# Start of a fused pooled attention and two MLPs: attention of nine subtiles in fp32, value sums on GpSimd, one table of preparation

## The chip, the cores and the metric

The kernel runs on one core of one Trainium2 chip. The metric is the device time of one execution in microseconds; a program's time is the median of its runs.

## The reference

Attention with pooled keys and values over 8 batches of 8 heads, then two MLPs over all 4608 tokens:

```
k_p = k.reshape(B, H, S // 8, 8, D).mean(axis=3)          # B 8, H 8, S 576, D 64
v_p = v.reshape(B, H, S // 8, 8, D).mean(axis=3)
attn = softmax(q @ k_p.T / sqrt(D));  x = attn @ v_p       # x: 4608 x 512
h = x @ w_in                                               # w_in 512 x 2048
g = where(h >= 1, h, where(h <= -1, 0, (h + 1) ** 2 / 4))
y = g @ w_out                                              # w_out 2048 x 512
h2 = y @ w_in2;  out = (h2 * sigmoid(h2)) @ w_out2
```

q, k and v are fp32, the four weights are 64-bit and are converted on the chip.

## The kernel before, in words

Products of the MLPs are made of three f16 products each (`three`, L121: high by high, high by low, low by high), so every weight and every activation is held as a high and a low f16 part. A *split* (L348) makes the two: ScalarE writes the high part (L349), VectorE the low part (L350).

The 4608 tokens are worked on in nine tiles of 512, and a tile's attention in four *subtiles* of 128 tokens. A batch has 576 tokens, so subtiles 0 to 8 (1152 tokens) are those of batches 0 and 1, and subtile 4 has tokens of both. A subtile passes five stages: `att_qT` (queries transposed, L523), `att_scores` (L546), `att_norm` (softmax, L585), `att_T` (transposed weights, L601) and `att_pv` (output, split into x of its tile, L632).

Before the change the first four subtiles (i < NI = 4) go in fp32: TensorE transposes queries and weights by the identity (L529, L607), multiplies with fp32 keys (L559) and fp32 sums of values (L647), and ScalarE copies the results from PSUM. All other subtiles go in f16: queries, keys, values and weights are split, and the queries, keys and weights are transposed by DMAs that SP issues (L544, L490, L612). For that the key sums and value sums of a batch need a mean (ScalarE, L448), a maximum over the partitions (`all_max`, L106: a product with the identity and a VectorE reduction), and a split (`batch_keys` L483, `batch_values` L499).

Sums over eight rows: keys of batch 0 by a VectorE reduction per head (L425), values of batch 0 by 64 products with the identity (L434) and one ScalarE copy (L439), the other batches by a DMA that accumulates, issued by GpSimd (`kv_more`, L412), and two VectorE additions (L442, L445).

A weight piece is read as raw 64-bit words. `look` takes its maximum (VectorE, L113), `scales` or `search` works out powers of two by a run of VectorE operations on a few columns (`w_scale` L167, `bits` L99), and the conversion is ScalarE L183, VectorE L95 and L191, ScalarE L261 (w_in) or L215 (w_out), a ScalarE cast to the high part (L263, L220) and a GpSimd subtraction for the low part (L264, L221). w_in has nine pieces, w_out four column blocks of two.

Tile 0 runs: attention of subtiles 0 to 3; 16 chunks of `emit_h` (L799, products `hps`) with their evacuation (ScalarE L817, VectorE L95, ScalarE L824, VectorE L828, then the split L856 and L857), whose results are all kept; then 4 x 16 steps of `yA` (L859, products `y`) that need the converted w_out blocks; then `evac_yA` (L876). Conversions, sums of batches 0, 1 and 2 and the attention of subtiles 4 to 7 are put between (L1108 to L1193). PSUM for attention is a ring of six buffers in the first part and of two (`ps_a`) after it (`att_ps`, L381).

The other tiles (L1214) do both MLP steps in one loop, with one or two steps of attention each turn and the second MLP's weights prepared beside. From L1270 the second MLP runs over tiles of 256 tokens.

The order on each engine: the code is traced in program order, and a planner that models the engines then lays out each engine's queue from it; each engine takes its queue in order. `behind(...)` (L128) keeps the instructions of a block from being laid out ahead of the latest *anchor* on the named engines. SP and GpSimd issue the DMAs.

Of the kernel before, what the change touches and what calls it, by code (L numbers as in the profile page):

```python
# [34 lines left out]
def tile_pooled_attention_two_mlps(  # L35
# [22 lines left out]
    POOL = 8  # L58
    SP = S // POOL
# [42 lines left out]

    ident = const.tile([128, 128], F32, name="ident")
# [57 lines left out]
    def all_of(m):  # L161

        g = sm.tile([128, 1], F32, tag="wg", name="wg", bufs=3)
        all_max(g, m)
        return g

    def w_scale(e, d, s, g, up=14):  # L167


        t = sm.tile([128, 8], F32, tag="wt", name="wt", bufs=2)  # L170
# [24 lines left out]
    def steps(piece, dst, scale, loaded, fill=None):  # L195
# [17 lines left out]
        def s3():  # L213
# [5 lines left out]
            hi, lo, *end = dst()  # L219
            nc.scalar.copy(out=hi, in_=x)  # L220
            nc.gpsimd.tensor_tensor(out=lo, in0=x, in1=hi, op=ALU.subtract)  # L221
            for f in end:
                f()
# [3 lines left out]
    def new_scale(e, g):  # L227
        ds = sm.tile([128, 2], F32, tag="ws", name="ws", bufs=3)
        w_scale(e, ds[:, 0:1], ds[:, 1:2], g)
        return ds[:, 0:1], ds[:, 1:2]  # L230

    def weight_in(w, e, tiles, cuts, rooms):
# [4 lines left out]
        mx, s, g, down = col(n), col(n), col(n), col(n)  # L237
# [16 lines left out]
        def work(p):  # L254
# [9 lines left out]
            nc.gpsimd.tensor_tensor(out=lo, in0=x, in1=hi, op=ALU.subtract)  # L264
# [39 lines left out]
    def weight_whole(w, e, fill, pieces):  # L304
# [16 lines left out]
        def scale():  # L321
            m = sm.tile([128, 1], F32, tag="wm1", name="wm1", bufs=3)
            nc.vector.tensor_reduce(out=m, in_=mx, axis=AX.X, op=ALU.max)
            w_scale(e, down, s, all_of(m), 12)
# [40 lines left out]
    SPT = (SP + 15) // 16 * 16  # L365
    v16 = [bp.tile([SP, 2, H, D], F16, name=f"v16{j}") for j in range(2)]
    e16 = [bp.tile([128, 2, 4, 128], F16, name=f"e16{j}") for j in range(2)]
# [6 lines left out]
    k32 = bp.tile([128, NP, 2, SP], F32, tag="kT", name="k32", bufs=2)  # L374
    nc.vector.memset(k32, 0.0)
    for x in e16:
        nc.gpsimd.memset(x, 0.0)
# [39 lines left out]

    def kv_pool(b, which, j):
        if j == 0:
# [3 lines left out]
        if (b, which) == (0, "k"):  # L423
            for h in (2 * j, 2 * j + 1):
                nc.vector.tensor_reduce(  # L425
                    out=sums[b, which][0:SP, h], in_=kv_raw.pop((b, which, h)).rearrange("p r d -> p d r"),
                    axis=AX.X, op=ALU.add,
                )
        elif b == 0:
            if j == 0:  # L430
                kv_raw["ps"] = att_ps([SP, H, D])
# [697 lines left out]
    r = XT[0]  # L1129
# [184 lines left out]
```

## Time and profile before

| | |
|---|---|
| median of 3 runs | 1617.79 us (1617.38 to 1619.02) |
| profiled execution | 1619.99 us, its span 1618.2 us |
| TensorE busy | 1535.0 us (95%) |
| VectorE busy | 1170.4 us (72%) |
| ScalarE busy | 898.9 us (56%) |
| GpSimd busy | 563.2 us (35%) |
| DMA | 166.35 MB, mean 103 GB/s |

PE is TensorE (PEld its weight load), DVE VectorE, ACT ScalarE, POOL GpSimd, SP the queue that issues most DMAs. A row's L number is a line of the kernel; a helper has one line for all that call it, so rows are told apart by their tiles as well. TensorE is busy nearly all the time from about 280 us on; the part before that is where the share is lower.

### The profile page before, as it was taken

To read this page: it belongs to the slowest core of one execution; us is meant where nothing else is said; L and a number is where in the kernel's file an instruction comes from. 1 tells how busy PE (TensorE), PEld (TensorE's weight loads), DVE (VectorE), ACT (ScalarE), POOL (GpSimd) and SP (SyncE) were. 2 spreads that over 40 slices of the span, in tenths; PEclk is the share of its full clock that TensorE was granted. 3 is DMA by queue.
4 is the path that set the end of the run, shared out by engine and by line. 5 is a ranking of instruction groups with operands and counts; after the bars stand their busy time and mean duration, and the time that the engine had idled before them with its cause. 6 is when DMAs were issued, how large, how long until landed. Compare 5 with 4: busy or idle time off the path is not lost.

```text
span 1618.2 us, 34378 instructions
## 1 busy us (share of the span) xinstructions
PE 1535.0 (95%) x14278; PEld 1060.2 (66%) x14278; DVE 1170.4 (72%) x2154; ACT 898.9 (56%) x1418; POOL 563.2 (35%) x508
## 2 busy tenths in 40 slices
PE   6846789999999999999999999999999999999998
PEld 6522344444444444444444489999999999999998
DVE  5798668676767677766757667777777777777765
ACT  2686565556666675664666555444455444555543
POOL 2314431214324333221555333343443333443322
PEclk9887799999999999999999999999999999999999
DMA  9635989957759576447583330100000100000000
GB/s 294 129 84 127 169 161 191 175 123 137 143 105 172 108 144 116 108 100 193 165 317 134 127 131 28 35 33 28 28 28 28 36 33 28 28 28 29 28 15 28
DMA packets 226157, 166.35 MB, mean 103 GB/s; under 512 B 154960, under 2 KB 193616, under 8 KB 226000
## 3 DMA queue, kind: packets, MB, share of 16 engines
q1 hardware_dynamic: 216592, 155.88, 37.8%
q0 software_dynamic: 9408, 8.27, 4.1%
q8 instruction: 112, 1.84, 0.5%
q14 instruction: 45, 0.37, 0.1%
HBM read 102.76 MB, written 33.55 MB: 84 GB/s over the span
## 4 chain that ended last, share of the span: by engine, by line
PE 56%; DVE 12%; issue 9%; ACT 8%; DMA 7%; POOL 7%; SPq 1%; DVEq 0%; POOLq 0%; ACTq 0%
PE y L122 6%; PE y L124 6%; PE y L123 6%; PE hps L123 5%; PE hps L124 5%; PE hps L122 5%; POOL c L714 4%; PE y L1018 3%; PE y L1020 3%; PE y L1019 3%; PE hb L123 3%; PE hb L122 3%; PE hb L124 3%; DMA yin<-y 3%; DVE g L350 2%
## 5 line engine op out<-in xcount | busy, mean ns | idle before, releaser
L124 PE MATMUL hb<-xh,wc 128*128 128x128 f16 x2016 | 347.7, 219 | 0.0
L122 PE MATMUL hb<-xh,wc 128*128 128x128 f16 x2016 | 347.7, 219 | 0.0
L123 PE MATMUL hb<-xl,wc 128*128 128x128 f16 x2016 | 347.7, 219 | 0.0
L350 DVE SCALAR_TENSOR_TENSOR g<-c,small,g 128x512 f16<-128x512 f32 x252 | 228.6, 910 | 94.4 <-ACT g L349 94.4
L1018 PE MATMUL y<-wd,g 128*128 128x256 f16 x1008 | 274.9, 273 | 1.7 <-DVE ob L1031 1.6
L1020 PE MATMUL y<-wd,g 128*128 128x256 f16 x1008 | 274.9, 273 | 0.0
L1019 PE MATMUL y<-wd,g 128*128 128x256 f16 x1008 | 274.9, 273 | 0.0
L958 ACT ACTIVATE c<-c,small 128x512 f32<-128x512 f32 x144 | 103.2, 717 | 230.4 <-DVE c L955 230.4
L122 PE MATMUL y<-g,wb 128*128 128x512 f16 x544 | 210.2, 387 | 19.9 <-ACT wb L220 19.9
L349 ACT ACTIVATE g<-c,small 128x512 f16<-128x512 f32 x252 | 177.6, 718 | 85.7 <-POOL c L717 48.2
L122 PE MATMUL hps<-xh,wa 128*128 128x512 f16 x576 | 219.9, 382 | 4.3 <-ACT wa L263 1.8
L123 PE MATMUL hps<-xl,wa 128*128 128x512 f16 x576 | 220.1, 382 | 1.4 <-DVE xl L350 1.4
L124 PE MATMUL hps<-xh,wa 128*128 128x512 f16 x576 | 219.6, 382 | 1.2 <-POOL wa L264 1.2
L124 PE MATMUL y<-g,wb 128*128 128x512 f16 x544 | 209.8, 386 | 3.6 <-POOL wb L221 3.6
L123 PE MATMUL y<-g,wb 128*128 128x512 f16 x544 | 210.3, 387 | 1.0 <-DVE g L857 1.0
L123 PEld LDWEIGHTS <-wc 128*128 128x128 f16 x2016 | 197.1, 98 | 2.4
L122 PEld LDWEIGHTS <-wc 128*128 128x128 f16 x2016 | 197.1, 98 | 2.2
L955 DVE TENSOR_TENSOR c<-c,hb 128x512 f32<-128x512 f32 x252 | 168.2, 682 | 41.5 <-PE hb L124 39.3
L124 PEld LDWEIGHTS <-wc 128*128 128x128 f16 x2016 | 197.1, 98 | 0.0
L828 DVE SCALAR_TENSOR_TENSOR g<-g,small,u 128x512 f32<-128x512 f32 x144 | 126.4, 878 | 61.8 <-ACT u L824 59.9
L593 POOL TENSOR_TENSOR e<-e,den 128x576 f32<-128x576 f32 x36 | 53.1, 1475 | 324.6 <-DVE den L592 234.5
L714 POOL TENSOR_TENSOR c<-c 128x512 f32<-128x512 f32 x108 | 163.9, 1532 | 2.8
(171 smaller groups left out, 2683.1 us busy)
## 6 DMA issues: line engine op xcount, KB each, us to landing
raw<-in_moe_w_out_dram SPq DMA_DIRECT2D x21, 1024.0 KB
raw<-in_moe_w_in_dram SPq DMA_DIRECT2D x18, 1024.0 KB
y<-y SPq DMA_DIRECT2D x36, 256.0 KB
yin<-y SPq DMA_DIRECT2D x18, 512.0 KB
out_dram<-ob SPq DMA_DIRECT2D x36, 256.0 KB
d<-hl SPq DMA_DIRECT2D x32, 256.0 KB
qt<-in_q_dram SPq DMA_DIRECT2D x31, 256.0 KB
wc<-d SPq DMA_DIRECT2D x8, 896.0 KB
```

What stands on the lines that cost most here:

```text
L122: nc.tensor.matmul(out=acc, lhsT=wh, rhs=xh, start=start, stop=False)
L123: nc.tensor.matmul(out=acc, lhsT=wh, rhs=xl, start=False, stop=False)
L124: anchor["pe"] = nc.tensor.matmul(out=acc, lhsT=wl, rhs=xh, start=False, stop=stop)
L349: a = nc.scalar.activation(out=hi, in_=x, func=AF.Copy, scale=s)
L350: return a, nc.vector.scalar_tensor_tensor(out=lo, in0=x, scalar=s, in1=hi, op0=ALU.mult, op1=ALU.subtract)
L714: nc.gpsimd.tensor_tensor(out=out, in0=a, in1=b, op=ALU.subtract)
L828: anchor["dve"] = nc.vector.scalar_tensor_tensor(out=g32_t[s], in0=g32_t[s], scalar=r["br"], in1=u_t.pop(s), op0=ALU.subtract, op1=ALU.max)
L955: nc.vector.tensor_tensor(out=out, in0=x, in1=y, op=ALU.add)
L958: nc.scalar.activation(out=x, in_=x, func=AF.Silu, scale=r["c1"])
L1018: nc.tensor.matmul(out=acc, lhsT=xh, rhs=wh, start=start, stop=False)
L1019: nc.tensor.matmul(out=acc, lhsT=xh, rhs=wl, start=False, stop=False)
L1020: nc.tensor.matmul(out=acc, lhsT=xl, rhs=wh, start=False, stop=stop)
```

## The change

- Subtiles 0 to 8 (`NE = 2 * S // 128 = 9`) go in fp32, not 0 to 3. Batch 1 gets fp32 keys (`keys32(1)`, a second `k32`), and the sums of values of batches 0 and 1 stay fp32, in the room of `v16`. `batch_keys` and `batch_values` of batches 0 and 1 fall away. The room of `e16` serves as a third buffer of `e` for subtiles 2 and 5.
- Batch 0's values are summed by GpSimd in three halvings for each half of the heads, traced at the first step; key heads 3 and 6 likewise.
- 16 products of the identity with itself are traced ahead of everything else on TensorE.
- Small columns (scales and maxima of w_in's pieces, `e1`, `wt`, `den`, `ch`) lie two columns apart.
- The preparation of tile 0 (looks, scales, conversions, sums of batch 1, w_out steps, attention slots) is put by tables of steps, `tick`. Three low halves (w_in pieces 3 and 7, w_out piece 0) are subtracted by VectorE. The first 40 attention slots of the later loop get `behind`.
- `cyb` shares the room of `m1`; `wm1` too.

```diff
+    WARM = 16
+    V0_AT = 0
+    VM_AT = 3
+    K_POOL = (3, 6)
+    LOOK_AT = [-6, -5, -4, -4, -3, -3, -2, -2, -1]
+    SCALE_AT = [-6, -3, -2, -1]
+    C1_AT = [-6, -3, -2, 2, 2, 3, 4, 10, 12]
+    B1_AT = [3, 4, 5, 6, 11]
+    MORE2_AT = 13
+    W2_AT = [[7, 10, 12, 13, 17, 18], [19, 19, 19, 19, 19, 19], [21, 21, 21, 21, 23, 23], [27, 27, 27, 27, 27, 27]]
+    SLOTS_AT = [9, 10, 12, 13, 14, 17, 18, 19, 20, 20, 23, 24, 28, 29, 30, 31, 31, 31, 31, 32]
+    HELD = 40
+    LO1 = (3, 7)
+    LO2 = (0,)
...
-    cols, free = const.tile([128, 96], F32, name="cols"), iter(range(96))
+    cols, free, free2 = const.tile([128, 136], F32, name="cols"), iter(range(46)), iter(range(45))
+    spread = cols[:, 46:136].rearrange("p (n u) -> p n u", u=2)
...
+    def apart(n):
+        i = [next(free2) for _ in range(n)][0]
+        return spread[:, i:i + n, 0]
...
+    def halving(to, r):
+
+        plus(r[:, 0:4], r[:, 0:4], r[:, 4:8])
+        plus(r[:, 0:2], r[:, 0:2], r[:, 2:4])
+        plus(to, r[:, 0], r[:, 1])
...
-            for n in range(POOL):
-                nc.tensor.matmul(
-                    out=ps[:, 2 * j:2 * j + 2], lhsT=ident[0:SP, 0:SP], rhs=r[:, :, n], start=n == 0,
-                    stop=n == POOL - 1,
-                )
-            if j == 3:
-                nc.scalar.copy(out=sums[b, which][0:SP], in_=kv_raw.pop("ps"))
+            if j < 2:
+                r = kv_raw.pop((b, which, j)).rearrange("p h r d -> p r h d")
+                halving(sums[b, which][0:SP, 4 * j:4 * j + 4], r)
...
-            for p in range(2 * hf, 2 * hf + 2) if i < NI else ():
-                nc.tensor.matmul(
-                    out=ps[:, p % 2 * 2:p % 2 * 2 + 2], lhsT=qT[:, p], rhs=k32[:, p], start=True, stop=True
-                )
+            for p in range(2 * hf, 2 * hf + 2) if i < NE else ():
+                for o, n, b, _ in segs(i):
+                    nc.tensor.matmul(
+                        out=ps[o:o + n, p % 2 * 2:p % 2 * 2 + 2], lhsT=qT[:, p, o:o + n], rhs=k32[b][:, p],
+                        start=True, stop=True,
+                    )
...
+    def warm(n):
+        ps = att_ps([128, 128])
+        for _ in range(n):
+            nc.tensor.matmul(out=ps, lhsT=ident, rhs=ident, start=True, stop=True)
...
     kv_load(0, "k")
+    warm(WARM)
...
+    def tick(n):
+        for f in steps_at.get(n, ()):
+            with behind("pe", "act", "dve"):
+                f()
+        if n >= 0:
+            slots_to(sum(a <= n for a in SLOTS_AT))
...
+        tick(n - 8)
...
-        2: lambda: keys_mean(0), 3: lambda: batch_keys(0), 4: lambda: batch_values(0), 5: lambda: sums_of(1, "k"),
-        6: lambda: keys_mean(1), 7: lambda: batch_keys(1), 8: lambda: sums_of(1, "v"),
-        9: lambda: values_mean(1), 10: lambda: batch_values(1),
...
+        tick(s + 1)
     new_acc(0)
     for d in range(KD):
-        if d + 1 < KD:
-            for n in range(6):
-                w2step(d + 1, n)
         for m in range(KF):
-            if m % 4 == 3:
-                slots_to(4 + 4 * d + m // 4 + 1)
+            if m % 4 == 0:
+                tick(KF + 3 + 4 * d + m // 4)
             yA(m, d, m == 0, m == KF - 1)
```

## Rows read from the trace of the kernel before

**Rows 1.** Windows: stretch, length, busy us (x instructions) by engine, granted clock, DMA share, GB/s.

```profile
0.00:60.00 60.00, 42.90 (x233) 36.97 (x234) 37.75 (x82) 21.77 (x33) 12.02 (x19) 0.96 0.98 256
60.00:127.00 67.00, 41.90 (x178) 18.25 (x176) 59.84 (x105) 56.18 (x80) 17.77 (x11) 0.81 0.42 107
127.00:215.00 88.00, 65.80 (x431) 30.01 (x432) 62.02 (x145) 48.76 (x77) 37.47 (x26) 0.79 0.73 137
215.00:300.00 85.00, 78.14 (x527) 37.90 (x524) 67.88 (x160) 49.77 (x88) 19.96 (x20) 0.96 0.91 183
300.00:950.00 650.00, 645.14 (x4012) 311.11 (x4011) 451.84 (x854) 398.09 (x652) 226.68 (x230) 1.00 0.62 148
950.00:1618.00 668.00, 661.11 (x8910) 625.94 (x8907) 491.05 (x812) 324.34 (x492) 249.26 (x204) 1.00 0.09 30
```

**Rows 2.** Timeline, 0 to 60 us: start, us, engine, line, operation, idle before.

```profile
5.85 0.35 PE L469 MATMUL att<-ident,sum 72*128 72x72 f32 x1 [5.85 <-DVE sum L425]
...
19.64 1.11 PE L529 MATMUL early<-ident,q 128*128 128x128 f32 x4 [0.76 <-DMA q<-in_q_dram]
...
28.06 13.88 PE L434 MATMUL att<-v,ident 72*72 72x128 f32 x64
...
42.93 0.46 DVE L568 TENSOR_REDUCE mx<-early 128x4 f32<-128x288 f32 x1 [6.94 <-PE early L559]
...
47.33 0.69 ACT L349 ACTIVATE xh<-att,small 128x512 f16<-128x512 f32 x1 [0.53 <-DVE den L589]
...
59.85 1.01 PE L122 MATMUL hps<-xh,wa 128*128 128x512 f16 x2 [1.25 <-ACT xh L349]
```

**Rows 3.** Waits of PE, 60 to 215 us: total us, times, longest.

```profile
PE y L122 <- ACT wb L220: 19.9, 2, 14.9
```

**Rows 4.** The chain that ended last, 60 to 215 us: start, us, what.

```profile
155.76 9.27 DMA aT<-e
...
165.94 2.32 SPq L544
...
169.00 11.93 DMA qT<-rows
```

**Rows 5.** Groups by line on POOL, 0 to 215 us: busy us, mean ns, idle before.

```profile
L264 POOL TENSOR_TENSOR wa<-xf,wa 128x1024 f16<-128x1024 f32 x7 | 16.1, 2296 | 16.5 <-ACT wa L263 16.4
L593 POOL TENSOR_TENSOR e<-e,den 128x576 f32<-128x576 f32 x8 | 10.0, 1251 | 60.4 <-DVE den L592 43.3 <-DVE eq L95 16.7 <-DVE wt L97 0.4
```

**Rows 6.** Groups by line on DVE, 60 to 215 us.

```profile
L350 DVE SCALAR_TENSOR_TENSOR krows<-sum,skv,krows 80x512 f16<-80x512 f32 x3 | 2.5, 838 | 0.9 <-ACT krows L349 0.9
```

**Rows 7.** Timeline: attention products in fp32 and f16, and f16 products of the MLP.

```profile
21.48 1.33 PE L559 MATMUL early<-k,qT 128*128 128x144 f32 x4
...
47.56 0.66 PE L647 MATMUL early<-aT,sum 72*64 72x128 f32 x8
...
49.08 1.04 PE L607 MATMUL early<-ident,e 128*72 128x128 f32 x8
...
147.48 0.69 PE L554 MATMUL att<-kT,qT 128*128 128x72 f16 x16 [0.28 <-DMA qT<-rows]
...
203.73 0.86 PE L647 MATMUL att<-aT,v 72*64 72x128 f16 x24
...
700.85 0.38 PE L124 MATMUL y<-g,wb 128*128 128x512 f16 x1
...
702.57 0.38 PE L123 MATMUL y<-g,wb 128*128 128x512 f16 x1
```

**Rows 8.** Timeline: small VectorE operations that start while GpSimd runs.

```profile
61.99 2.43 POOL L264 TENSOR_TENSOR wa<-xf,wa 128x1024 f16<-128x1024 f32 x1 [4.88 <-ACT wa L263]
62.35 2.10 DVE L97 TENSOR_SCALAR wt<-cols 128x3 f32<-128x3 f32 x1
...
130.23 2.57 POOL L264 TENSOR_TENSOR wa<-xf,wa 128x1024 f16<-128x1024 f32 x1
130.74 0.20 DVE L95 TENSOR_SCALAR wm<-wm 128x1 f32<-128x1 f32 x1
```

More of the change, by code (lines that the diff above doesn't have):

```diff
@@ L236, in weight_in @@
         held, n = {}, len(cuts)
-        mx, s, g, down = col(n), col(n), col(n), col(n)
+        mx, s, g, down = (apart(n) for _ in range(4))
         def load(p):
@@ L373, in tile_pooled_attention_two_mlps @@
     nc.gpsimd.memset(vm, FLOOR * POOL / (H * D))
[L374 to L377, printed above, removed]
+    k32 = [bp.tile([128, NP, 2, SP], F32, tag="kT", name="k32", bufs=2) for _ in range(2)]
+    nc.vector.memset(k32[0], 0.0)
+    nc.gpsimd.memset(k32[1], 0.0)
     early = {"n": 0, "on": True}
@@ L492, in values_mean @@
     def values_mean(b):
-        sums_mean(sums[b, "v"][0:SP], vm, v16[b % 2])
+        junk = v16[b % 2] if b > 1 else ap.tile([SPT, H, 2, D], F16, tag="krows", name="by", bufs=2)[0:SP]
+        sums_mean(sums[b, "v"][0:SP], vm, junk)
     def values_scale(b):
@@ L534, in att_qT @@
             return
-        e, s = (sm.tile([128, 1], F32, tag=n, name=n) for n in ("eq", "sq"))
-        c = cq_t[i] = sm.tile([128, 1], F32, tag="cq", name="cq", bufs=3)
+        c = sm.tile([128, 3], F32, tag="cq", name="cq", bufs=3)
+        e, s, c = (c[:, j:j + 1] for j in range(3))
+        cq_t[i] = c
         x = rows(128)
@@ L552, in att_scores @@
                 for o, n, b, _ in segs(i):
-                    for j in range(2) if i >= NI else ():
+                    for j in range(2) if i >= NE else ():
                         nc.tensor.matmul(
@@ L595, in att_norm @@
         )
-        for hf, x in enumerate(e16 if i >= NI else ()):
+        for hf, x in enumerate(e16 if i >= NE else ()):
             x, y = x[:, :, :, 0:SP], e[:, 4 * hf:4 * hf + 4]
@@ L776, in small @@
     def small(**names):
-        x = sm.tile([128, sum(names.values())], F32, tag="t" + "".join(names), name="small", bufs=3)
-        r, a = {}, 0
+        wide = names.pop("ch", 0)
+        x = sm.tile([128, sum(names.values()) + 2 * wide], F32, tag="t" + "".join(names), name="small", bufs=3)
+        r, a = {"ch": x[:, 0:2 * wide].rearrange("p (n u) -> p n u", u=2)[:, :, 0]}, 2 * wide
         for n, w in names.items():
@@ L1201, in next_slot @@
     def next_slot():
-        slots_left.pop(0)()
+        if len(slots_left) > NTOKS - HELD:
+            with behind("pe", "act", "dve"):
+                slots_left.pop(0)()
+        else:
+            slots_left.pop(0)()
         q_to(2 * NI + (NTOKS - len(slots_left)) // 4 + 3)
```

139 lines of the change are left out of this document (66 added, 73 removed).

## Prediction

> **What bounds the kernel now.** I read the windows view first, cut at the points where the work changes: the attention of the first token tile (0 to 60 us), the first half of tile 0's network (60 to 127), its second half (127 to 215), tile 1 (215 to 300), the other tiles (300 to 950), the second network (950 to 1618) [rows 1]. From 300 us on TensorE is busy for 645.14 of 650 and 661.11 of 668 us at a granted clock of 1.00. The diff touches that part only in small columns, so what is won or lost before 300 us should reach the end one for one. Before 300 us TensorE is idle for 17.1, 25.1, 22.2 and 6.9 us of the four stretches, and its granted clock is 0.81 and 0.79 in the two that hold tile 0. That is the room: some 71 us idle, and products that run at half speed for part of the time.
>
> Next, what ended the idle time. In the first stretch the values of batch 0 are summed by 64 identity products, 13.88 us on TensorE [rows 2]. The scores of subtile 3 stand behind them in TensorE's queue, so VectorE sits idle for 6.94 us; the first split of x starts at 47.33 and the first product of tile 0, released by the last split, at 59.85. In the second stretch VectorE is busy 59.84 of 67 us and ScalarE 56.18 [rows 1]: these two are the bound, and TensorE waits 19.9 us in all for the w_out pieces that ScalarE converts [rows 3]. In the third the chain of waits goes through DMA transposes: 9.27 us for aT, a 2.32 us issue on SP, 11.93 us for qT [rows 4].
>
> **The change, part by part.**
>
> *Values' sums on GpSimd.* Off TensorE go 64 products and one ScalarE copy. On go six GpSimd adds in two halvings of 1024, 512 and 256 elements per partition. A 1024-element GpSimd operation takes 2.30 us as a mean [rows 5]; halved twice, 1.15 and 0.6 as estimates, so 2 x 4.1 = 8.2 us. They wait for v, which SP issues before the fourth q load; that q is there at 19.64 [rows 2], so the sums end at about 19.6 + 4.1 + two softmax multiplications (2.5 [rows 5]) = 26, or at 31 if nothing overlaps. From the end of the sums (41.94) to the first split of x (47.33) was 5.4 us, so that split moves to 33 to 37. The key heads 3 and 6 go to GpSimd too, about 2 x 1 us beside VectorE's other six: a microsecond or two at the front, hidden behind the loads, and I take nothing. GpSimd's queue now has these adds ahead of the softmax multiplications and of the second pair of key and value DMAs that it issues; the estimate of 31 has that.
>
> What is late next? The loads. k, v, four q and the first weight come to about 11.8 MB, and the stretch moved 256 GB/s at a share of 0.98 [rows 1]: 46 us as an estimate for the last piece, and its maximum must be known before the first evacuation, though not before the first products. VectorE has 37.75 us of work in 60 there, so it can have the four subtiles done by then. I put the first product at 47, **-13 us**. Ends: 0, if the last split stays where it was, behind the weight's conversion in ScalarE's queue; -18, at the end of the old value sums.
>
> *Products of the identity first.* Sixteen 128x128 fp32 products; four such took 1.11 us [rows 2], so 4.4 us. TensorE was idle until 5.85 [rows 2], waiting for key sums. Hidden; nothing gained if the clock has fallen again before tile 0, at most 2 us (half of the few microseconds of attention products that follow) if not; if the cover goes, +1. I take 0.
>
> *Preparation by one table.* In the second stretch the conversions keep their cost and change their places. Batches 0 and 1 lose four splits of keys and values on VectorE, 0.84 us each [rows 6], with their maxima, some 5 us; on ScalarE the means, splits and copies of the same. The scales and two conversions move ahead into the first stretch, where VectorE has 22 us idle [rows 1]: some 5 us. Against that VectorE takes three low halves from GpSimd (the nearest row, a split of 512 elements with two inputs in SBUF, takes 0.84 [rows 6], so 0.8 + 2 x 1.6 = 4 us) and about one attention subtile earlier, 3 us. The stretch shrinks by what VectorE loses on balance, between 3 us (10 less 7) and 10 (if the added work fits in its idle time); I take **-6**. A wait is added: batch 1's key sums now come at step 2 of the loop and not 5. If the accumulating DMA has not landed, VectorE stands with tile 0's evacuations queued behind it, and TensorE runs out of PSUM. The buffers are free 14 us earlier because the value sums are, which should cover it: 0, at worst +10 (three steps of 12 products and their waits).
>
> *Subtiles 4 to 8 in fp32.* SP loses 5 qT, 10 aT and 4 kT transposes. The two in the chain with the issue between are 23.5 us [rows 4]. TensorE instead does, per subtile, four transposes (1.11), four score products (1.33), eight transposes (1.04) and eight output products (0.66): 4.1 us against 0.69 + 0.86 = 1.55 for f16 [rows 2, 7]. That is +2.6 each, 10 for subtiles 4 to 7, and 2.6 for subtile 8, which lies in tile 1. Bottom up, the third stretch needs 192 products, and at full speed eight of them start in 1.72 us, 0.215 apart [rows 7] (41.3 us), what is left of the attention (2.7 subtiles x 4.1 = 11), small maxima (2): 54. It took 88. I allow 14 us for waits on w_out, whose second piece is started only when the output products start, so 68: **-20 us**. Ends: -33 with no waits; -8 if half of the time that the transposes held goes to waits of TensorE on ScalarE's copies. In tile 1 subtile 8's 2.6 stands against two fewer DMA waits: **0**, from -4 to +3.
>
> *Small columns apart.* A VectorE operation on three adjacent columns took 2.10 us when a GpSimd subtraction had started before it, and ended as that ended; one on a single column, under another GpSimd subtraction, took 0.20 [rows 8]. The maxima, scales and denominators of the change lie two columns apart, and no row shows such an operation. Ends: 0, if several columns wait wherever they lie; -5, the 1.9 us of this one and a like amount for the denominators and constants of tile 0. The two rows differ in whether a second column lies beside the first, and apart none does, so I take the side of the free one, with part of it off the path: **-3**.
>
> The Trainium skill (VectorE: DVE Perf Modes, "What auto-detection actually checks") lets an fp32 operation with one source use both ports when source and destination are in SBUF and their outermost counts are even or equal, and asks nothing of the step there. By that rule columns two apart would still be held and the sum would have 0 for -3; the blocked row agrees with it, and no row tests the step.
>
> **Sum.** 13 + 6 + 20 + 3 = 42 us off the profiled execution's 1619.99 (span 1618.2, 1.8 around it) gives 1578. That execution lies 2.2 us above the median of the runs, 1617.79, so against the median I forecast **1576 us**.
>
> **The rivals.**
> 1. *VectorE and ScalarE stay the bound.* They were busy 89% and 84% of the second stretch [rows 1]; if the work moved ahead of it only queues up in the first, and the w_out conversions pace the third, the gain is 13 + 0 + 8 = 21: 1597. For it: the 19.9 us of waits on ScalarE [rows 3]. Against: VectorE was idle for 22 us in the first stretch and 26 in the third.
> 2. *Slower, by the PSUM ring.* After tile 0's attention all attention products share a ring of two PSUM buffers. An fp32 subtile takes six turns of it (qT, two scores, two transposes, one output), an f16 one three. TensorE's queue is in order, so each turn may hold the products behind it until ScalarE or VectorE has emptied a buffer. That is 15 added turns for five subtiles. It decides from 42 / 15 = 2.8 us a turn; at 3.5 it costs 52 and gives 1628. For it: VectorE and ScalarE are 70% and 55% busy in the third stretch [rows 1], with long conversions in front. Against: where TensorE waited for a split of ScalarE's it was 1.25 us [rows 2].
> 3. *The stages run at the engines' own pace.* -18, -10, -33 and -3 for the columns less 3 for turns of the ring: 1557. For it: no DMA left in tile 0's attention chain. Against: every piece has to be handed through four engines.
> 4. *Columns apart are held like adjacent ones.* All else as forecast, 0 for -3: 1579. For it: the only row of several columns under GpSimd is held. Against: the single column that is not.
> 5. *It does not do what it says:* the table changes places in program order, but each engine's queue is still laid out by the planner; if that lays them out as before, and the fp32 products eat what the transposes gave back, the time stays within 3 us.
>
> **How the numbers follow.** Forecast 0.39; rival 1 0.17; rival 2 0.10; rival 3 0.10; rival 4 0.20; rival 5 0.04. What a measurement can tell from no change is about 0.2%, 3.2 us. Faster: 0.39 + 0.17 + 0.10 + 0.20 = 0.86; same 0.04; slower 0.10. The range runs from rival 3 to a little beyond rival 1: 1556 to 1603; it leaves out rivals 2 and 5 (0.14) and the far tail of rival 3. The forecast's own range, by bounds that do not all fall on one side, is 1563 to 1592.
>
> **What would show it.** First product of tile 0 at about 47 us, no VectorE idle of 7 us before it; the tile's last evacuation near 176 and not 215; no DMA transpose in the chain between 100 and 180; TensorE's idle time before 300 us some 35 to 40 and not 71; granted clock above 0.9 in the output products. Small operations on columns apart of 0.3 us or less while GpSimd runs speak against rival 4. If the first product stays near 59, the first term is wrong; if TensorE waits on the att copies grow to tens of microseconds, rival 2; if VectorE is above 90% busy and TensorE waits on w_out, rival 1. Products after 300 us that are no longer back to back would overturn the frame itself.

## The result and the profile after

The changed kernel takes 1579.47 us (median of 4 runs, 1578.03 to 1581.64) against 1617.59 for the kernel before beside it (4 runs, 1616.8 to 1619.02): **ratio 0.9759, 95% interval 0.9744 to 0.9773**, 38 us less. The forecast was 1576, 0.974 of the kernel before. The profiled execution took 1581.64 us, its span 1579.8. The total was right; none of its four terms came out at its size.

The windows of the kernel after, at the same cuts as [rows 1] (length, busy us by engine, granted clock, DMA share, GB/s):

```profile
0.00:60.00 60.00, 45.22 (x247) 31.98 (x248) 46.69 (x100) 25.98 (x37) 30.68 (x36) 0.77 1.02 261
60.00:127.00 67.00, 47.66 (x207) 22.43 (x206) 63.55 (x97) 56.09 (x80) 18.09 (x10) 0.85 0.63 137
127.00:215.00 88.00, 83.29 (x476) 43.37 (x475) 64.29 (x138) 51.19 (x74) 24.23 (x16) 0.96 0.53 123
215.00:300.00 85.00, 85.00 (x612) 41.92 (x611) 70.43 (x164) 53.98 (x95) 23.02 (x24) 1.00 0.95 186
300.00:950.00 650.00, 645.27 (x4261) 328.94 (x4259) 460.58 (x850) 401.26 (x650) 238.71 (x232) 1.00 0.58 142
```

TensorE's idle time before 300 us fell from 71 to 38.8 us (14.8, 19.3, 4.7 and 0); from 215 to 300 us it does not stand at all. From 300 to 950 us TensorE is as busy as before (645.27 against 645.14 us), so the frame of the forecast holds, within some microseconds that the runs below show. The largest change is in the third window: from 65.80 busy at a clock of 0.79 to 83.29 at 0.96.

The timeline of the kernel after, first stretch:

```profile
16.44 2.35 POOL L121 TENSOR_TENSOR v<-v 72x1024 f32<-72x1024 f32 x1 [4.75 <-DMA v<-in_v_dram]
20.03 4.79 POOL L121 TENSOR_TENSOR v<-v 72x1024 f32<-72x1024 f32 x3 [1.25 <-DMA v<-in_v_dram]
...
28.45 1.91 PE L643 MATMUL early<-ident,e 128*72 128x128 f32 x8
...
45.66 0.58 PE L147 MATMUL hps<-xh,wa 128*128 128x512 f16 x1 [1.03 <-ACT xh L371]
```

GpSimd now sums the values, twice held by their transfer, and the first product stands at 45.66 us, 14.2 earlier than in [rows 2]. But the first *output* product came at 125.58 before (at the end of the 14.9 us wait of [rows 3]) and comes at 122.24 now: of the 14 us, 3 are left there. The two marks are not the same point of the work, though. In the kernel before, the first output products stood ahead of the last two of the 16 chunks, whose w_in piece ScalarE cast to its high part only at 128.66 us:

```profile
128.66 1.03 ACT L263 CAST wa<-xf 128x1024 f16<-128x1024 f32 x1
...
135.51 0.38 PE L122 MATMUL hps<-xh,wa 128*128 128x512 f16 x1
```

In the kernel after, that piece is cast at 106.00 and all chunks come ahead of the output products. The last product of the chunks started at 140.7 before and starts at 113.4 now, 27.3 us earlier. The other marks are the evacuations of the accumulators at the end of tile 0 and of tile 1. Groups of that ScalarE line in the kernel after:

```profile
L922 ACT ACTIVATE y<-y,cy x2: 679/683/687, 183.8 to 184.4; 128x512 f32<-128x512 f32 x2
...
L922 ACT ACTIVATE y<-y,cy x2: 667/677/687, 286.1 to 288.1; 128x512 f32<-128x512 f32 x2
```

The same line started at 214.7 and 322.3 us in the kernel before. So tile 0 ends 30.9 us earlier, tile 1 takes 102.3 instead of 107.6 (another 5.3), and the other 2.2 of the 38.4 us between the two spans come later. These marks are used for every run below.

TensorE's waits of the kernel after, 60 to 215 us (total, times, longest):

```profile
PE hps L147 <- ACT wa L285: 8.1, 2, 7.4
PE att L643 <- POOL e L629: 4.9, 1, 4.9
PE y L149 <- POOL wb L246: 2.9, 1, 2.9
...
PE y L147 <- ACT wb L245: 0.3, 1, 0.3
```

The 19.9 us for ScalarE's w_out pieces [rows 3] are gone. In the chain that ended last, 45 to 190 us, no DMA transpose is left [rows 4]; instead it has the transfer and the sums of batch 1:

```profile
53.18 13.06 DMA raw<-in_k_dram
66.34 1.22 DVE raw L468
...
76.12 6.37 DVE raw L468
...
123.27 7.16 DMA raw<-in_moe_w_out_dram
```

### The profile page after: what moved, and what is told of

Same layout as the page of the kernel before. It is cut to its first block, busy times and chain, and to the rows that moved or that the text cites. A ratio compares the mean times of both kernels' runs of the same rounds, so it can differ in the third digit from the quotient of the medians.

```text
span 1579.8 us, 34130 instructions
## 1 busy us (share of the span) xinstructions
PE 1530.5 (97%) x14210; PEld 1060.0 (67%) x14210; DVE 1172.5 (74%) x2120; ACT 894.4 (57%) x1397; POOL 568.9 (36%) x507
## 4 chain that ended last, share of the span: by engine, by line
PE 82%; DVE 7%; DMA 4%; ACT 4%; issue 2%; POOL 1%; SPq 1%; DVEq 0%; ACTq 0%; POOLq 0%
PE hb L149 7%; PE hb L147 7%; PE hb L148 7%; PE y L1051 7%; PE y L1053 7%; PE y L1052 7%; PE y L147 6%; PE y L149 6%; PE y L148 6%; PE hps L148 6%; PE hps L147 6%; PE hps L149 6%; PE att L685 1%; DVE xf L216 1%; DVE g L861 1%
## 5 line engine op out<-in xcount | busy, mean ns | idle before, releaser
L149 PE MATMUL y<-g,wb 128*128 128x512 f16 x544 | 207.6, 382 | 4.0 <-POOL wb L246 2.9
L148 PE MATMUL y<-g,wb 128*128 128x512 f16 x544 | 208.0, 382 | 1.0 <-DVE g L890 1.0
L147 PE MATMUL y<-g,wb 128*128 128x512 f16 x544 | 208.1, 383 | 0.3 <-ACT wb L245 0.3
L850 ACT ACTIVATE g<-hps,small 128x512 f32<-128x512 f32 x144 | 111.2, 773 | 80.8 <-PE hps L149 74.2
```

The lines of the kernel that those rows point to most:

```text
L147: nc.tensor.matmul(out=acc, lhsT=wh, rhs=xh, start=start, stop=False)
L148: nc.tensor.matmul(out=acc, lhsT=wh, rhs=xl, start=False, stop=False)
L149: anchor["pe"] = nc.tensor.matmul(out=acc, lhsT=wl, rhs=xh, start=False, stop=stop)
L850: nc.scalar.activation(out=w, in_=h_t.pop(s), func=AF.Relu, scale=c_A(r, "c1", s), bias=r["br"])
```

## The experiments

The theory after the result was that the change is a sum of four terms as forecast. The rival was that one term carries most of it and the others are hidden. First each part was set back by itself. Differences in us are differences of two ratios to the kernel before, times 1618; each ratio's interval is about 0.0015 to either side, so such a difference is good to some 3.4 us.

**Values' sums back on TensorE** (`values_pe`):

```diff
-    V0_AT = 0
+    V0_AT = 3
...
-            if j < 2:
-                r = kv_raw.pop((b, which, j)).rearrange("p h r d -> p r h d")
-                halving(sums[b, which][0:SP, 4 * j:4 * j + 4], r)
...
+            for n in range(POOL):
+                nc.tensor.matmul(
+                    out=ps[:, 2 * j:2 * j + 2], lhsT=ident[0:SP, 0:SP], rhs=r[:, :, n], start=n == 0,
+                    stop=n == POOL - 1,
+                )
+            if j == 3:
+                nc.scalar.copy(out=sums[b, which][0:SP], in_=kv_raw.pop("ps"))
```

> The changed kernel with one part undone: batch 0's values are summed by 64 identity products on TensorE again, traced at the fourth step as before. Theory A (the parts add up, as forecast): the first product of tile 0 moves back from 45.7 to some 57 to 60 us and the time rises by about 13 us, to 1592. Theory B (VectorE's and ScalarE's work decides when the output products can start, in both kernels near 125 us, so the early start is given back in the second stretch): the first product moves back all the same, but the first output product stays within 3 us of 125 and the time is 1579 to 1584.

Measured: 0.9775 (0.9759 to 0.9791), 2.6 us over the kernel after and not to be told from it. The first product did not move back. Timeline of this run:

```profile
17.15 3.03 PE L467 MATMUL early<-v,ident 72*72 72x128 f32 x26 [0.73 <-PE early L596]
...
20.63 3.88 PE L467 MATMUL early<-v,ident 72*72 72x128 f32 x34
...
43.64 0.59 PE L147 MATMUL hps<-xh,wa 128*128 128x512 f16 x2 [0.27 <-ACT xh L371]
```

(The code has 32 products here; the trace has two records of each fp32 product that is not a transpose, and the 64 are records.) With four more at 25 us the 64 take 7.5 us, not the 13.88 of [rows 2], start 11 us earlier, and the first product comes 2 us sooner than with GpSimd's sums. So in the changed kernel, with the products of the identity in place, GpSimd's sums buy nothing at the front.

**Subtiles 4 to 8 back in f16** (`f16_again`; their keys, values and transposes as before, the table kept but for the steps of the sums, which are nine again and not five):

```diff
-    B1_AT = [3, 4, 5, 6, 11]
+    B1_AT = [3, 4, 5, 6, 7, 8, 9, 10, 11]
...
-    NE = 2 * S // 128
+    NE = NI
...
-    B1 = [lambda: sums_of(1, "k"), lambda: keys32(1), lambda: sums_of(1, "v"), lambda: values_mean(1),
-          lambda: values_scale(1)]
+    B1 = [lambda: keys_mean(0), lambda: batch_keys(0), lambda: batch_values(0), lambda: sums_of(1, "k"),
+          lambda: keys_mean(1), lambda: batch_keys(1), lambda: sums_of(1, "v"), lambda: values_mean(1),
+          lambda: batch_values(1)]
```

> The changed kernel with one part undone: subtiles 4 to 8 go in f16 again, with DMA transposes and with the splits of keys and values of batches 0 and 1; the table keeps its places. Theory A (the transposes held the third stretch): DMA transposes are in the chain between 120 and 190 us again and the time rises by 20 us or more, to 1600 or above. Rival (the table and the value sums made the gain, and fp32 only trades DMA waits for 13 us of TensorE work): 1575 to 1586.

Measured: 0.9797 (0.9783 to 0.9812), 6.1 us over the kernel after. Tile 0's last evacuation is at 182.8 us, no later than with fp32; tile 1 takes 109.1 us instead of 102.3. But the added steps put batch 1's sums at steps 6 and 9, later than in the kernel after, and this alone is worth 5.2 us (`sums_late`, below). Against that run, which has the sums at the same two steps, f16 costs 11.3 us: tile 0 ends 4.9 us later (177.9 there), and tile 1 takes 6.7 us longer. The cause in tile 1 stands in TensorE's waits from 180 us on, and in the chain there.

```profile
PE att L581 <- DMA qT<-rows: 7.1, 1, 7.1
```

```profile
201.86 14.87 DMA qT<-rows
```

**The old table in the changed kernel** (`table_old`: the four lists from step 2 on; those of the attention ahead of tile 0 are the same in both). The old code put the batch sums and w_out at the end of a step, and its number plus one is that place in the table. It put the conversions at the start of a step, so their entries here are one step late; and it held them only behind the splits of x, where the table holds them behind the latest anchors of three engines:

```diff
-    C1_AT = [-6, -3, -2, 2, 2, 3, 4, 10, 12]
-    B1_AT = [3, 4, 5, 6, 11]
-    W2_AT = [[7, 10, 12, 13, 17, 18], ..., [21, 21, 21, 21, 23, 23], ...]
-    SLOTS_AT = [9, 10, 12, 13, 14, 17, 18, 19, 20, 20, 23, 24, 28, 29, 30, 31, 31, 31, 31, 32]
+    C1_AT = [-6, -3, -2, 5, 7, 8, 9, 11, 13]
+    B1_AT = [6, 7, 9, 10, 11]
+    W2_AT = [[7, 8, 10, 11, 12, 14], ..., [23, 23, 23, 23, 23, 23], ...]
+    SLOTS_AT = [15, 16, 17, 18, 20, 21, 22, 23, 24, 25, 26, 27, 28, 29, 30, 31, 32, 33, 34, 34]
```

> The changed kernel with the table's places put back to those of the kernel before (conversions of w_in pieces 3 to 8, sums of batch 1, w_out steps, attention slots); all other parts stay. Theory A: the table is worth the 6 us of the forecast, 1585. Theory B (VectorE's load alone counts, not its order): 1579 within 2 us. Theory C (without the earlier attention slots the fp32 products come too late): 1595 or more.

Measured: 0.9932 (0.9918 to 0.9947), **28 us over the kernel after**. The first product stands at 45.37 and the first output product at 122.10, as in the kernel after; tile 0's last evacuation is at 212.5, 2.2 us before that of the kernel before. Window and waits of this run (127 to 215, and 60 to 215 us):

```profile
127.00:215.00 88.00, 67.56 (x385) 35.73 (x383) 46.47 (x110) 39.71 (x55) 25.12 (x16) 0.86 0.35 78
```

```profile
PE hps L147 <- ACT wa L285: 11.1, 4, 4.9
PE all L129 <- DVE wm L109: 10.6, 2, 6.4
PE y L147 <- ACT wb L245: 8.3, 3, 5.6
PE y L149 <- POOL wb L246: 6.1, 2, 5.3
```

TensorE stands 20 us there while no other engine is busy for more than 46.47 of 88: what is missing is not capacity but the next step's place in the queues. The 28 us are the price of these lists, not quite of the old places.

**The fp32 subtiles alone, in the kernel before** (`fp32_alone`; with the second `k32` and the fp32 sums of values, as in the change):

```diff
+    NE = 2 * S // 128
...
-        if i < NI:
+        if i < NE:
...
-        2: lambda: keys_mean(0), 3: lambda: batch_keys(0), 4: lambda: batch_values(0), 5: lambda: sums_of(1, "k"),
-        6: lambda: keys_mean(1), 7: lambda: batch_keys(1), 8: lambda: sums_of(1, "v"),
-        9: lambda: values_mean(1), 10: lambda: batch_values(1),
+        5: lambda: sums_of(1, "k"), 6: lambda: keys32(1), 8: lambda: sums_of(1, "v"),
+        9: lambda: values_mean(1), 10: lambda: values_scale(1),
```

> The kernel before with one part added: subtiles 4 to 8 in fp32, batch 1's keys in fp32, no splits for batches 0 and 1; value sums on TensorE, old places, adjacent columns, no products ahead. Theory A: the transposes leave the chain and the time falls by 20 to 28 us from 1617.6, to 1590 to 1598. Rival (PSUM ring and TensorE work eat most of it): 1605 to 1615.

Measured: 0.9963 (0.995 to 0.9976), 6 us less than before; tile 0's last evacuation at 209.9. The transposes are gone, but its waits of TensorE, 60 to 215 us, keep the old first row nearly whole, 19.2 against 19.9 us [rows 3]:

```profile
PE y L122 <- ACT wb L220: 19.2, 2, 13.6
```

So fp32 is worth 6 us in the old kernel, 4.8 of it by the end of tile 0, and 11 in the new one with the sums in the same places. The next four runs took the table apart.

**Only the conversions' list set back** (`conversions_old`, the `C1_AT` line of the diff above):

> The changed kernel with one list of its table set back: conversions 3 to 8 of the first weights at their old steps. The whole table set back took 1.7% of the kernel before (0.9759 to 0.9932, some 28 us), where the forecast had 6. Theory 'weights': the products stood for the late conversions in that run (wait for ACT wa 11.1 us and for POOL wa 4.3 us between 60 and 127 us, against 8.1 and 2.7 us after), so this list alone carries most of it: ratio 0.985 to 0.990, and the products of the first weights last until about 135 us again. Rival 'slots': the six conversions only move waits about in a stretch that VectorE and ScalarE fill anyway: 0.976 to 0.979.

Measured: 0.9839 (0.9823 to 0.9854), 12.9 us over. The first output product comes at 130.78 instead of 122.24, after more waiting for w_in pieces (60 to 215 us):

```profile
PE hps L147 <- ACT wa L285: 15.2, 3, 6.6
```

In the kernel before this wait was 1.8 us in all (the products of the last piece stood behind output products there):

```profile
PE hps L122 <- ACT wa L263: 1.8, 1, 1.8
```

So the run does not bring the old places back. ScalarE cast pieces 3 to 7 of w_in ahead of evacuations 1, 3, 5, 5 and 6 of the chunks in the kernel before; it casts them ahead of evacuations 4, 5, 6, 7 and 13 in the kernel after, and ahead of 7, 7, 9, 9 and 13 here. The cast of piece 4:

```profile
72.72 0.60 ACT L263 CAST wa<-xf 128x512 f16<-128x512 f32 x1
```

in the kernel before, and here

```profile
78.41 0.62 ACT L285 CAST wa<-xf 128x512 f16<-128x512 f32 x1
```

though the first product of the chunks stands 15 us earlier. The 12.9 us are what this delay costs; what the change gained over the old places of the conversions was not measured, and in ScalarE's order it moved them back, not forward.

**Only the attention slots' list set back** (`slots_old`, the `SLOTS_AT` line):

> The changed kernel with the other large list set back: the attention slots of the second group of subtiles at their old steps, one per step, all inside the output products of tile 0. Theory 'slots': with the whole table set back TensorE stood 20 us between 127 and 215 us (28 us of that stretch, the clock 0.86 against 0.96) while no other engine was busy more than 46 of 88 us, so the slots' chains among the output products are the loss: ratio 0.984 to 0.990, tile 0's last evacuation at 195 to 210 us against 184, tile 1's first products behind it. Rival 'weights': the slots find room beside the output products: 0.976 to 0.979.

Measured: 0.9873 (0.9856 to 0.989), 18.4 us over; the first output product is on time (122.71), the last evacuation at 202.3. The window that loses, and the two waits in it by their total:

```profile
160.00:200.00 40.00, 25.48 (x136) 13.97 (x135) 15.86 (x35) 13.12 (x19) 11.65 (x9) 0.74 0.47 93
```

```profile
PE y L147 <- ACT wb L245: 12.8, 2, 7.1
...
PE y L149 <- POOL wb L246: 6.2, 1, 6.2
```

Both lists carry a loss, one ahead of the output products and one among them; only the slots' is measured against the old places.

**Only batch 1's sums late** (`sums_late`):

```diff
-    B1_AT = [3, 4, 5, 6, 11]
+    B1_AT = [6, 7, 9, 10, 11]
```

> The changed kernel with batch 1's sums and scales at their old steps 6, 7, 9, 10, 11 instead of 3 to 6 and 11. The forecast priced the early place at 0, at worst 10 us. Theory 'held': the trace of after has the early key sums in its chain at 66.3 us and 76.1 us, the second held to 6.4 us under two GpSimd operations, with the conversions of the first weights queued behind them on VectorE, so later sums gain 2 to 6 us: 0.972 to 0.975. Rival 'needed': subtiles 4 to 8 need these keys by the new slots' places, from step 9 on, so that late sums hold the attention of tile 1 up: 0.978 to 0.985. Neither: within 0.1% of after.

Measured: 0.9727 (0.9712 to 0.9741), **5.2 us less than the kernel after, and the fastest version of this study**; tile 0 ends at 177.9, tile 1 at 280.3. On the same chip the run with the columns side by side, whose order on every engine is that of the kernel after, took 1579.36 to 1582.28 us, this one 1575.47 to 1577.85. The timelines show the price of the early places. Kernel after:

```profile
69.30 4.47 POOL L286 TENSOR_TENSOR wa<-xf,wa 128x512 f16<-128x512 f32 x1 [10.54 <-ACT wa L285]
...
76.05 6.45 DVE L468 TENSOR_TENSOR raw<-raw 72x1024 f32<-72x1024 f32 x1
76.44 4.96 POOL L286 TENSOR_TENSOR wa<-xf,wa 128x1024 f16<-128x1024 f32 x2
```

With the late sums:

```profile
68.58 1.62 POOL L286 TENSOR_TENSOR wa<-xf,wa 128x512 f16<-128x512 f32 x1 [9.52 <-ACT wa L285]
73.57 2.13 POOL L286 TENSOR_TENSOR wa<-xf,wa 128x1024 f16<-128x1024 f32 x1 [3.37 <-ACT wa L285]
...
77.17 1.21 DVE L468 TENSOR_TENSOR raw<-raw 72x1024 f32<-72x1024 f32 x1
77.35 3.69 POOL L286 TENSOR_TENSOR wa<-xf,wa 128x1024 f16<-128x1024 f32 x1 [1.65 <-ACT wa L285]
...
85.95 1.21 DVE L468 TENSOR_TENSOR raw<-raw 72x1024 f32<-72x1024 f32 x1
```

The addition at 76.05 is that of batch 1's values; in the late run it stands at 85.95 (the one at 77.17 is that of the keys). It takes 1.21 us there and 6.45 here, while two GpSimd subtractions run, and the evacuations of tile 0 queue behind it. GpSimd's low half at 69.30, for which products wait, takes 4.47 instead of 1.62 beside a run of VectorE's conversions and evacuations. The Trainium skill (GPSIMD Engine Reference, "8. Key points") says that GpSimd shares its SBUF interfaces with VectorE and contends with VectorE instructions that have two SBUF inputs; the row of 6.45 us, an addition of two SBUF tensors, agrees. Which of the two is held differs: the addition at 77.17 overlaps a subtraction too and takes its 1.21 us, while the subtraction takes 3.69 instead of 2.13. That the held addition is the whole price is not shown: in `values_pe`, with the early sums, it took 1.21 us, and late sums still gained 3.1 us there (0.9775 to 0.9756, `late_pe_values`), though that is within what such a difference is good to.

**Batch 1's sums between** (`sums_mid`):

```diff
-    B1_AT = [3, 4, 5, 6, 11]
+    B1_AT = [5, 6, 9, 10, 11]
```

> The changed kernel with batch 1's sums and scales at steps 5, 6, 9, 10, 11, between the changed table (3, 4, 5, 6, 11) and the old one (6, 7, 9, 10, 11). With the old places the products waited 2.7 us for the keys' copies on ScalarE at 88 us. Theory 'first GpSimd, then VectorE': what cost was the key sums among the conversions at 66 to 82 us, so step 5 still pays part of it: 0.973 to 0.976. Rival: the values' sums at steps 5 and 6 were the cost and the keys are better early: 0.970 to 0.973.

Measured: 0.9736 (0.9719 to 0.9752), tile 0 at 179.5. It lies between the two others, 1.5 us from `sums_late`, too close to rank the steps of the keys against those of the values by their times. Tile 0 has 4.3 of the 5.9 us with the values' sums at step 9 and the keys' at 5.

**Columns side by side** (`columns_adjacent`, the same queues on every engine):

```diff
-    spread = cols[:, 46:136].rearrange("p (n u) -> p n u", u=2)
+    spread = cols[:, 46:136].rearrange("p (u n) -> p n u", u=2)
...
-        den = sm.tile([128, H, 2], F32, tag="den", name="den")[:, :, 0]
+        den = sm.tile([128, 2, H], F32, tag="den", name="den")[:, 0]
```

> The changed kernel with its small columns side by side again; the same instructions in the same order on every engine. The forecast gave the columns apart 3 us (0.2%): 0.978. Rival (columns apart are held like adjacent ones): the trace of after has operations on columns apart held to 2.12, 3.98 and 3.47 us under GpSimd operations, so nothing changes: 0.975 to 0.977, and operations on 128x3, 128x8 and 128x9 columns under GpSimd take as long as in after.

Measured: 0.9753 (0.9738 to 0.9768), the kernel after's time. VectorE's small operations under GpSimd, in the kernel after, two columns apart:

```profile
48.45 3.26 POOL L286 TENSOR_TENSOR wa<-xf,wa 128x1024 f16<-128x1024 f32 x1 [8.65 <-ACT wa L285]
49.61 2.12 DVE L111 TENSOR_SCALAR wt<-wt 128x3 int32<-128x3 int32 x1
```

and side by side:

```profile
49.04 3.26 POOL L286 TENSOR_TENSOR wa<-xf,wa 128x1024 f16<-128x1024 f32 x1 [9.17 <-ACT wa L285]
50.22 2.11 DVE L111 TENSOR_SCALAR wt<-wt 128x3 int32<-128x3 int32 x1
```

The attention's denominators (128x8) tell the same: 3.47 us apart, 3.52 side by side, under the same two GpSimd subtractions of 5.00 us.

**Without the products of the identity** (`no_identity`):

```diff
-    warm(WARM)
```

> The changed kernel without its sixteen products of the identity at the start. The forecast gave them 0: 0.975 to 0.977. Theory 'nothing left to warm': in the trace of after the products between 26 and 40 us are slow all the same (8 transposes of the attention take 1.9 to 2.3 us, against 1.1 to 1.2 in the run with values' sums on TensorE), and the queries' transfer ends the wait at 20.8 us, so the first product stays at 45 to 46.5 us and the time within 0.1% of after. Rival 'clock': the early transposes and scores run at half speed and push the chain before 20 us on: first product at 48 us or later, 0.977 to 0.980.

Measured: 0.9764 (0.9746 to 0.9781), the kernel after's time within its interval. The front is even earlier in this run:

```profile
28.55 1.07 PE L643 MATMUL early<-ident,e 128*72 128x128 f32 x8
...
42.55 0.58 PE L147 MATMUL hps<-xh,wa 128*128 128x512 f16 x1 [1.13 <-ACT xh L371]
```

but its three microseconds go at once: from 60 to 215 us TensorE waits 12.9 us for the w_in pieces that ScalarE converts, against 8.1 after, and tile 0 ends at 183.9.

**Both off: values on TensorE, no identity** (`pe_values_no_identity`, the two edits together):

> The changed kernel with values' sums of the first batch on TensorE again and without the products of the identity. With these products and the sums on TensorE the 64 products of the sums took 7.5 us and the first product of the weights stood at 43.6 us; in the kernel before they took 13.9 us, 217 ns each. Theory 'identity first': what took the 14 us out of the front is the clock that the products of the identity raise, not the move of the sums, so without both the 64 products take 13 to 14 us again and the first product of the weights stands at 50 to 58 us: ratio 0.981 to 0.987. Rival 'table and GpSimd's key sums': the front is early for other reasons (keys' sums shared by two engines), and the 64 products keep the clock up by themselves once they start: first product by 46 us, 0.976 to 0.979.

Measured: 0.9806 (0.9787 to 0.9825), 7.6 us over the kernel after. The timeline:

```profile
26.44 7.15 PE L467 MATMUL att<-v,ident 72*72 72x128 f32 x64
...
50.46 1.01 PE L147 MATMUL hps<-xh,wa 128*128 128x512 f16 x2 [0.45 <-ACT xh L371]
```

Neither theory is right: the first product is late, as the first said, but the 64 records stand 112 ns apart without the identity products, not 217 as in the kernel before. What is lost is their place: they start at 26.44 and not at 17.15 us. Behind 40 us TensorE is slower too: sixteen records of the attention's output at 42.16 took 1.98 us, and in `values_pe` at 37.79 they took 1.09.

The 217 and the 112 ns go with TensorE's granted clock. `fp32_alone`, whose front is that of the kernel before, had the 64 in 13.88 us as well. Its window around them, and that of this run:

```profile
28.00:42.00 14.00, 14.00 (x67) 14.00 (x67) 7.58 (x15) 4.75 (x7) 4.34 (x3) 0.50 1.10 353
```

```profile
26.00:34.00 8.00, 8.00 (x76) 8.00 (x75) 7.83 (x19) 3.54 (x5) 2.31 (x2) 1.00 1.07 371
```

So they ran at the lower of the clock's two levels, 1.2 GHz, in the old front and at 2.4 GHz here. The trace of the kernel before shows 1.00 for the same 28 to 42 us, with the same 14.00 us busy; the spacing of 217 ns speaks against it, and the 0.96 of the first stretch in [rows 1] is not to be relied on.

**Late sums with values on TensorE** (`late_pe_values`):

> The changed kernel with two of its edits set back: values' sums on TensorE and batch 1's sums at their old steps (the identity products stay). If the two are independent, by their single runs: 0.9727 plus 0.0015, so 0.972 to 0.975. If TensorE's sums also keep the clock up for the stretch behind (tile 0's last evacuation stood at 179.3 us in that run against 183.8 after, with the early sums still in), the gain shows in tile 0: evacuation at 173 to 176 us and 0.969 to 0.972, the fastest so far.

Measured: 0.9756 (0.974 to 0.9773), a miss: no faster than the kernel after, though tile 0 ends at 176.9, the earliest of all. Tile 1 takes 105.4 us, 3 more than with the late sums alone; its f16 subtiles now wait for a transpose, and the granted clock from 177 to 283 us is 0.98 against 1.00:

```profile
PE att L692 <- DMA aT<-e: 1.4, 2, 1.2
```

Against the late sums alone some more microseconds are lost behind tile 1. All runs show such a step: from tile 1's last evacuation to the end the span has 1292.8 to 1294.6 us in the nine kernels whose values of batch 0 GpSimd sums, and 1295.9 to 1299.4 in the five where TensorE does (one profile each). So the 2.6 us of `values_pe` lie behind tile 1 and not at the front, where TensorE's sums were the faster; why is open.

The marks side by side, each read from its run's trace (us):

| kernel | ratio | first product | last product of the chunks | first output product | tile 0 ends | tile 1 ends |
|---|---|---|---|---|---|---|
| before | 1 | 59.85 | 140.7 | 125.58 | 214.7 | 322.3 |
| after | 0.9759 | 45.66 | 113.4 | 122.24 | 183.8 | 286.1 |
| values_pe | 0.9775 | 43.64 | 110.2 | 118.31 | 179.3 | 282.8 |
| f16_again | 0.9797 | 43.35 | 113.3 | 121.82 | 182.8 | 291.9 |
| table_old | 0.9932 | 45.37 | 137.2 | 122.10 | 212.5 | 315.3 |
| fp32_alone | 0.9963 | 59.58 | 135.8 | 121.12 | 209.9 | 314.7 |
| conversions_old | 0.9839 | 44.98 | 123.2 | 130.78 | 196.5 | 298.1 |
| slots_old | 0.9873 | 45.03 | 112.1 | 122.71 | 202.3 | 304.7 |
| sums_late | 0.9727 | 45.28 | 110.7 | 118.68 | 177.9 | 280.3 |
| pe_values_no_identity | 0.9806 | 50.46 | 115.1 | 124.59 | 189.5 | 290.4 |

## Why the prediction was right in sum and wrong in its terms

The parts set back one at a time cost 2.6 us (values' sums), 0.8 (identity), 28.0 (table), 6.1 (fp32) and -1.0 (columns): 36.5 against 39.0 for the whole (1 less 0.9759, times 1618). The forecast had 13, 0, 6, 20 and 3. That the parts come near the whole does not show that they are additive: the first two cost 3.4 singly and 7.6 together, the 28.0 is for conversions later than the old ones, and the 6.1 has the gain of later sums in it. From the other side, `fp32_alone` and `pe_values_no_identity` differ by 25.4 us; that is the table, the columns, and the small parts that no run took by itself (two key heads on GpSimd, three low halves on VectorE, the third buffer of `e`, `behind` for the later slots). So the table is worth some 20 us more than forecast, values' sums, fp32 and columns together some 17 to 28 less, and that the two errors cancelled to within 3.5 us of the time is luck. Point by point:

- **Values' sums, -13.** The first product came at 45.66, forecast 47. But the step "that split moves to 33 to 37", because TensorE no longer does the sums, was not what mattered: with the sums back on TensorE it stood at 43.64, and with the identity products gone as well at 50.46. The term's mistake was to take [rows 2]'s 13.88 us as what the sums cost; at the clock's upper level they cost 7.2 to 7.5. The two parts stand in for each other: each alone is worth 3 us or less, both together 7.6. Of the way from 59.58 in `fp32_alone` to 50.46 without either, 6.7 us are the clock's level under the sums; what raised it there was not tried.
- **"Won before 300 us reaches the end one for one."** True of the end of tile 1 within some 4 us: `values_pe` ends it 3.3 us before the kernel after and takes no less in all. False of a gain in an earlier stage. With the front 14 us earlier, the last product of the fourteenth chunk still starts at 106.3 us, against 102.4 before. VectorE is busy for 63.55 of 67 us in that stretch, which is rival 1's mechanism. What was won lies in the last two chunks, whose w_in piece comes 22.7 us earlier. With the old lists the same early front gave 2.2 us at tile 0's end. A gain in front of a stage is kept only if the steps that the stage waits for move too.
- **The table, -6.** Mis-sized by some 20 us. The forecast looked at the second stretch and counted VectorE's work; it also had scales and two conversions move into the first stretch, which the table does not do: its places before the first chunk are the old ones. What is shown to be worth something lies behind, the attention slots (18.4), against batch 1's sums, which give back 5.2. The conversions' gain is not shown (`conversions_old`). The w_out list was not tried by itself, but the traces point at it: the last w_in piece was cast at 128.66 us before, at 124.03 with all old lists, at 113.88 with the conversions alone set back, and at 106.00 after, where the w_out steps stand behind it.
- **The added wait, "0, at worst +10".** It costs 5.2 us. Not the transfer, which held VectorE for 1.0 us, but the work itself, of which the held addition (6.45 us instead of 1.21) is the part that the trace shows; the forecast had no thought of it. Such a price stood in [rows 8] for another operation.
- **fp32, -20.** Worth 6 to 11. The step that failed is the third stretch's 88 us put down to the transposes of [rows 4]: from the last product of the chunks to tile 0's end it is 74.0 us in the kernel before and 74.1 in `fp32_alone`, without the transposes of subtiles 4 to 7. The w_out waits of [rows 3] keep it there, 19.2 us where the forecast allowed 14 for waits. The 4.8 us that the old kernel does gain by tile 0's end come earlier, in the chunks. In the new kernel that stretch is 70.4 us, near the 68 of the forecast; with f16 again it is 69.5, and 67.2 in `sums_late`, which has the sums at the same steps. Subtile 8's "0, from -4 to +3" was low: in the new kernel tile 1 gains 6.7 from fp32.
- **The price of an fp32 subtile, 4.1 us.** Near by accident. The rows read as four score and eight output products are half of a subtile's records, eight and sixteen, and the transposes and scores among them ran at the lower clock. At the upper one the whole is some 4.0 us (0.66, 1.15, 1.07 and 1.09 in the traces of the changed kernels). The 192 products of the third stretch also left out the 24 of the last two chunks, which stood in it in the kernel before.
- **Products of the identity, 0.** Right as measured beside GpSimd's sums (0.8 us, within the interval); beside TensorE's sums they are worth 5.0 (0.9775 against 0.9806). The sixteen are 32 records and took 5.31 us, not the 4.4 worked out from four transposes.
- **Columns apart, -3.** Zero; rival 4 was right. The Trainium skill (VectorE: DVE Perf Modes, "What auto-detection actually checks") asks nothing of the step for one fp32 source in SBUF, and the trace agrees: 2.12 us apart, 2.11 side by side. Had the forecast followed it, its sum would have been 1579, the measured time.
- **Rival 2, the PSUM ring.** Not seen: TensorE's longest wait for a copy of attention results between 60 and 215 us is 0.6 us.

Of the signs named ahead, the first product (47, measured 45.66), the chain without transposes, the idle time (35 to 40, measured 38.8) and the clock (over 0.9, measured 0.96) came true, and the evacuation (176, measured 183.8) was late by 8, most of which tile 1 gave back. VectorE above 90% busy, a sign of rival 1, came true as well (63.55 of 67 us), but the waits on ScalarE's w_out pieces that go with it fell to 0.3 us. They could not tell the terms apart: nearly all of them are what any cause of a shorter third stretch would show.

## What to carry to other kernels

A wait on the critical chain is worth its length only if no other strand ends just behind it: look for the second row of waits before pricing the first. When several engines hand a stage on, moving the next steps earlier in the queues can be worth more than making any of them cheaper; here 18 us lay in the places of the attention slots alone, and no engine beside TensorE was busy for more than 45 of the 88 us from 127 on in the run that lost them. Price work added to VectorE by what GpSimd does at that moment, not by its duration elsewhere, and if a list of places was made as a whole, set its entries back one by one: one of them was a loss of 5 us. See in the trace that a run meant to restore an old order does: one of these did not, and another moved a second list along.

## What was not expected of the hardware

- Products of the identity at the start do not keep TensorE fast for long, and the run without them was the faster of the two later on. In the kernel after, eight transposes of the attention's weights at 28.45 us took 1.91 us; without the identity products eight such took 1.07 us at 28.55. In the windows from 30 to 35 us the granted clock is 0.50 with them and 1.00 without. With them four transposes of queries took 0.62 us at 10.94, without 1.06 at 9.84; at 20 to 21 us four took 0.66 in both, behind a wait of 3.5 to 3.8 us for queries. After that both were slow, one until 38 us and the other until 27. Why they differ there is open.
- The same 64 records took 13.88, 7.5 and 7.15 us in three kernels, 217 or 112 ns each, at a granted clock of 0.50 (in `fp32_alone`) or 1.00. Starting early or late did not decide it: they ran fast from 17 us and from 26 us, and slow from 28. What raised the clock in time in the one and not in the other is open.
- Where a VectorE addition of two SBUF tensors and GpSimd subtractions overlap, now the one and now the other takes longer: the addition 6.45 us against 1.21 in the kernel after, the subtraction 3.69 against 2.13 in `sums_late`.
